# Batch 0's score stacks in the x buffer of batch 1, and two more jobs that score on float32r parts

## The chip, the cores and the metric

The kernel runs on one core of one Trainium2 chip. The metric is the device time of one launch in microseconds, as the median of several runs. Names of engines: PE is TensorE, PEld its weight loads, DVE VectorE, ACT ScalarE, POOL GpSimd, SP SyncE, which issues most DMAs.

## What is computed

Attention with a forget gate over 4 batches, 8 heads, 576 tokens and a head width of 64, then two feed-forward layers over the 2304 tokens, 512 to 2048 to 512 wide. The core of the reference:

```python
scores = (1 / sqrt(64)) * q @ k.T
cum = cumsum(log(clip(f, 1e-4, 1)), axis=-1)
scores = where(causal, -1e9, scores + cum[..., :, None] - cum[..., None, :])
attn = exp(scores - max(scores)); attn = attn / (sum(attn) + 1e-9)
x = (attn @ v).transpose(0, 2, 1, 3).reshape(2304, 512)
h = x @ moe_w_in;  g = h * tanh(softplus(h));  x = g @ moe_w_out
h = x @ moe2_w_in; g = h * cos(h);             out = g @ moe2_w_out
```

Inputs are float32. The kernel keeps their accuracy in matmuls by splitting operands in a high and a low float32r part and summing products of parts.

## The kernel before

**Attention** is cut in jobs of two heads (a head pair). Batch 0 has eight jobs: jobs 0 to 3 are its four head pairs on query blocks 0 and 1 (256 queries, 256 keys), jobs 4 to 7 the same pairs on blocks 2, 3 and 4 (128, 128 and 64 queries, 384, 512 and 576 keys). The text numbers jobs from 0, so the seventh and eighth job are jobs 6 and 7, and job 8 is the first of batch 1. Batches 1 to 3 have four jobs each, with all five blocks. An item is a block of a job. `attention_units` (L365) runs over half items: scores of an item (`scores`, L513) and the weighted sum of an older one (`av`, L622) in the first half, transposes of the item three back (`transposes`, whose copies out of PSUM are L594 on ScalarE and L596 on VectorE) and the normalising (L575 on GpSimd) in the second. Row maxima are taken on VectorE (L558), exponentials on ScalarE (L562).

**Stacks.** A score matmul contracts 128 rows: 64 of q (or k), two rows of the cumulated gate, and constant rows of -1, 0 and 1 that add one and subtract the other. The operands of a job lie in a stack, of which there are two of each kind, used in turn by even and odd jobs. A plain stack is float32: one matmul per head and column range (L521), which runs as two passes. A float32r stack has four parts and takes two float32r matmuls (L527), the second of which adds the products with the low parts. In the kernel before `whole(jb)` says that all jobs of batch 0 are plain. `prep_job` (L430) fills the stack of the next job during the present one: DMAs of the gate rows from `cumd`, transposes by TensorE (L470), and copies out of PSUM. For a plain stack these are ScalarE copies (L494) and one on VectorE (L496). For a float32r stack each run of columns takes, for each head, a ScalarE copy (high part, L501) and a VectorE subtraction (low part, L502), and then a GpSimd copy that duplicates the high part (L507).

**Where the stacks lie.** The plain pair is in a pool of its own. The float32r stack of even jobs (`stkr0`, first used by job 8) lies in the attention pool from the start. The one of odd jobs takes the place of the plain pair: when job 9 is prepared, that pool is closed and the new stack is cleared by `new_stack` (L654) with six GpSimd memsets (L672 to L679), which wait for the last plain scores, those of job 7. In GpSimd's queue five of them stand ahead of the last duplicating copy for job 8.

**Around it.** Matmuls of the first layer's hidden units on finished tokens (`hidden_units`, L164, matmuls L159, copies L184 on ScalarE and L186 on VectorE) fill TensorE between attention's steps; a credit that grows per half item says how many. I call them fills. From the start w_in is converted piece by piece, on VectorE and ScalarE in turn (L127, L129, L135, L139, L141). After attention come the rest of the hidden units, the first layer's output and the second layer, all TensorE work. The order within each engine's queue is not the order of the code alone: the tile framework's list scheduler places each instruction by its own timeline, keeping dependences.

Of the kernel before, what the change touches and what calls it, by code (L numbers as in the profile page):

```python
# [9 lines left out]
F32 = mybir.dt.float32  # L10
# [17 lines left out]
CUT_BATCHES = (0,)  # L28
PAIR_LAG = 3
# [12 lines left out]
def tile_attention_two_ffn(  # L42
# [322 lines left out]
    def attention_units(p, bank):  # L365
# [13 lines left out]

        def span(jb):  # L380
            pi, bl = jobs[jb]
            return divmod(pi, NP) + (QS[bl[0]], QS[bl[-1]] + QR[bl[-1]], bl[-1])

        def load_job(jb):
# [37 lines left out]
        def part(jb, rows, x, j, lo, hi):  # L422
            st, tails = stack(jb)
            if whole(jb) or x % 2:
                return st[x][rows, j, lo:hi]
# [4 lines left out]
        def prep_job(jb):  # L430
# [6 lines left out]
            for row, x in ((96, 0), (64, 1)) if whole(jb) else ((96, 2), (64, 3)):  # L437
# [3 lines left out]
                elif whole(jb):  # L441
# [25 lines left out]
            for g in groups:  # L467
# [6 lines left out]
                for (which, P), run in runs.items():  # L474
# [12 lines left out]
                    if whole(jb):  # L487
# [25 lines left out]
        def scores(jb, i):  # L513
# [5 lines left out]
            def product(o, j, c0, c1):  # L519
                if whole(jb):  # L520
# [12 lines left out]
            if r == 64:  # L533
                heads.append([])
                for c0, c1, mk in ((0, w // 2, maskt[:, 0 : w // 2]), (w // 2, w, mask2[:, 320 - w // 2 : 320])):
                    t = bank()[:, 0 : c1 - c0]
                    for j in (1, 0) if whole(jb) else (0, 1):
                        with ExitStack() as hold:
                            if whole(jb) and j == 0:
                                hold.enter_context(tc.issue_after(marks["score"].ins))  # L540
                            product(t[64 * j : 64 * j + 64] if whole(jb) else t, j, c0, c1)
# [110 lines left out]
        stacks, early = {}, ExitStack()  # L652

        def new_stack(pool, name, dt, en):  # L654
            if dt == F32:
                t = pool.tile([128, 2, 2, S], dt, name=name, bufs=1)
                st, tails = [t[:, 0], t[:, 1]], None
                q, k = st
                nc.gpsimd.memset(q[96:128], 0.0)
                en.memset(q[64:96], -1.0)  # L660
            else:
                t = pool.tile([128, 2 * QW + 4 * S], dt, name=name, bufs=1)
                st, tails = [None] * 4, {}
                for n, x in enumerate((0, 2)):
                    at = n * QW
                    w = QW - TAIL
                    st[x] = t[:, at : at + 2 * w].rearrange("p (j s) -> p j s", j=2)[:, :, 0:TAIL]
                    at += TAIL
                    both = t[:, at : at + 256].rearrange("p (j s) -> p j s", j=2)[:, :, 0:64]
                    tails[x] = (t[:, at : at + 128], t[:, at + 64 : at + 192], both)  # L670
                    if n:
                        en.memset(f(t[64:96, n * QW : n * QW + QW]), -1.0)  # L672
                        nc.gpsimd.memset(f(t[96:128, n * QW : n * QW + QW]), 0.0)
                    nc.gpsimd.memset(f(t[:, at + 64 : at + 128]), 0.0)
                    at = 2 * QW + 2 * S * n
                    st[x + 1] = t[:, at : at + 2 * S].rearrange("p (j s) -> p j s", j=2)
                k = f(st[3])
            nc.gpsimd.memset(k[64:96], 0.0)
            en.memset(k[96:128], 1.0)  # L679
            return st, tails  # L680

        def stack(jb):
            key = (whole(jb), jb % 2)
            if key not in stacks:
                if key == (False, late % 2):
                    early.close()
                    pool = late_sb.enter_context(tc.tile_pool(name="stk", bufs=1))
                else:
                    pool = p
                stacks[key] = new_stack(pool, f"stkr{jb % 2}", F32R, nc.gpsimd)  # L690
# [229 lines left out]
```

## Time and profile before

| | us |
|---|---|
| median of 3 runs | 1022.57 (1022.57 to 1023.02) |
| profiled execution | 1022.4 |
| its span | 1020.6 |
| granted clock of TensorE, mean | 0.998 |
| TensorE busy | 998.3 (98% of the span) |
| VectorE busy | 582.3 |
| ScalarE busy | 539.0 |
| GpSimd busy | 178.6 |

The span is what the trace shows, from the first to the last instruction; the profiled execution has 1.8 us around it. TensorE's share is an average. Attention fills about the first third, and there the engines stand otherwise in each stage; a stage is read by a window of its own.

### The profile page before, as it was taken

To read this page: it belongs to the slowest core of one execution; us is meant where nothing else is said; L and a number is where in the kernel's file an instruction comes from. 1 tells how busy PE (TensorE), PEld (TensorE's weight loads), DVE (VectorE), ACT (ScalarE), POOL (GpSimd) and SP (SyncE) were. 2 spreads that over 40 slices of the span, in tenths; PEclk is the share of its full clock that TensorE was granted. 3 is DMA by queue.
4 is the path that set the end of the run, shared out by engine and by line. 5 is a ranking of instruction groups with operands and counts; after the bars stand their busy time and mean duration, and the time that the engine had idled before them with its cause. 6 is when DMAs were issued, how large, how long until landed. Compare 5 with 4: busy or idle time off the path is not lost.

```text
span 1020.6 us, 16522 instructions
## 1 busy us (share of the span) xinstructions
PE 998.3 (98%) x5852; PEld 855.8 (84%) x5852; DVE 582.3 (57%) x1350; ACT 539.0 (53%) x1158; POOL 178.6 (17%) x255
## 2 busy tenths in 40 slices
PE   5998999999999999999999999999999999999998
PEld 3686899899999999988898888888888888888887
DVE  5867766665555437657662487665544544444454
ACT  5885765665555446557664565544433333333343
POOL 7225432432332200012220031110000000000000
PEclk9999999999999999999999999999999999999999
DMA  5874333233322268848784546102101100100010
GB/s 122 215 205 113 99 88 99 72 95 90 88 71 60 67 224 285 272 139 306 241 293 122 178 147 246 42 1 83 42 1 58 68 1 1 51 32 1 1 42 21
DMA packets 118494, 111.77 MB, mean 110 GB/s; under 512 B 66700, under 2 KB 87180, under 8 KB 118412
## 3 DMA queue, kind: packets, MB, share of 16 engines
q1 hardware_dynamic: 114060, 106.00, 34.0%
q10 hardware_dynamic: 4352, 4.72, 1.4%
q8 instruction: 46, 0.75, 0.3%
q14 instruction: 36, 0.29, 0.1%
HBM read 77.49 MB, written 33.18 MB: 108 GB/s over the span
## 4 chain that ended last, share of the span: by engine, by line
PE 90%; DMA 3%; ACT 3%; POOL 2%; DVE 2%; issue 1%; SPq 0%; POOLq 0%; ACTq 0%; DVEq 0%
PE h L159 24%; PE acc L264 19%; PE hx L159 11%; PE acc L256 11%; PE hx L256 4%; PE h L256 4%; PE s L527 4%; PE s L637 4%; PE s L613 3%; DMA raw<-in_moe_w_in_dram 2%; PE acc L159 2%; PE s L470 2%; ACT s L562 1%; PE s L521 1%; PE s L601 1%
## 5 line engine op out<-in xcount | busy, mean ns | idle before, releaser
L159 PE MATMUL h<-xb,wih 128*128 128x288 f32 (+2 forms) x840 | 180.4, 303 | 2.1 <-DVE hs L186 1.0
L159 PEld LDWEIGHTS h<-xb,wih 128*128 128x128 f32 x840 | 136.2, 188 | 8.7 <-issue 2.1
L159 PE MATMUL h<-xb,wil 128*128 128x288 f32 (+2 forms) x420 | 124.4, 297 | 0.0
L575 POOL TENSOR_SCALAR s<-s,sm 128x128 f32<-128x128 f32 (+4 forms) x144 | 84.3, 598 | 183.0 <-DVE sm L573 121.4
L264 PE MATMUL acc<-woh,gh 128*128 128x512 f32 x288 | 112.9, 392 | 0.0
L264 PE MATMUL acc<-woh,gl 128*128 128x512 f32 x288 | 112.3, 391 | 0.0
L264 PE MATMUL acc<-wol,gh 128*128 128x512 f32 x288 | 112.0, 389 | 0.0
L562 ACT ACTIVATE s<-s,mx 128x128 f32<-128x128 f32 (+4 forms) x144 | 83.6, 581 | 46.4 <-DVE mx L558 45.3
L558 DVE CUSTOM_DVE_ANT_0 s<-s,maskt 128x128 f32<-128x128 f32 (+4 forms) x144 | 67.2, 483 | 55.0 <-PE s L613 24.3
L329 DVE TENSOR_TENSOR gl<-hl,gh 128x512 fp32r<-128x512 f32 x72 | 57.8, 803 | 69.1 <-ACT gh L324 68.8
L315 ACT ACTIVATE n<-n 128x512 f32<-128x512 f32 (+1 forms) x80 | 47.1, 589 | 86.6 <-DVE n L309 86.5
L159 PE MATMUL hx<-x,wih 128*128 128x512 f32 (+1 forms) x320 | 92.7, 369 | 0.0
L159 PE MATMUL h<-x,wih 128*128 128x512 f32 (+1 forms) x320 | 91.0, 369 | 0.0
L329 DVE TENSOR_TENSOR gl<-e,gh 128x512 fp32r<-128x512 f32 (+1 forms) x80 | 53.9, 674 | 51.7 <-ACT gh L324 51.6
L308 DVE TENSOR_SCALAR n<-e 128x512 f32<-128x512 f32 (+1 forms) x80 | 32.7, 408 | 85.3 <-ACT e L301 84.7
L159 PEld LDWEIGHTS h<-xb,wil 128*128 128x128 f32 x420 | 78.8, 188 | 0.8
L324 ACT ACTIVATE gh<-e 128x512 fp32r<-128x512 f32 (+1 forms) x80 | 47.1, 589 | 53.6 <-DVE e L320 50.0
L324 ACT ACTIVATE gh<-hl 128x512 fp32r<-128x512 f32 x72 | 45.1, 627 | 47.5 <-issue 30.2
L256 PE MATMUL acc<-gl,woh 128*128 128x512 f32 (+1 forms) x192 | 67.7, 354 | 0.0
L159 PEld LDWEIGHTS hx<-x,wih 128*128 128x128 f32 x320 | 58.4, 188 | 11.0
L256 PE MATMUL acc<-gh,wol 128*128 128x512 f32 (+1 forms) x192 | 67.6, 354 | 0.0
L159 PEld LDWEIGHTS h<-x,wih 128*128 128x128 f32 x320 | 58.4, 188 | 10.9
(121 smaller groups left out, 2119.7 us busy)
## 6 DMA issues: line engine op xcount, KB each, us to landing
hl<-hd SPq DMA_DIRECT2D x72, 256.0 KB
raw<-in_moe_w_in_dram SPq DMA_DIRECT2D x32, 512.0 KB
raw<-in_moe_w_out_dram SPq DMA_DIRECT2D x32, 512.0 KB
hd<-hs SPq DMA_DIRECT2D x32, 288.0 KB
yd<-stage SPq DMA_DIRECT2D x32, 256.0 KB
x<-yd SPq DMA_DIRECT2D x32, 256.0 KB
natk<-in_k_dram SPq DMA_DIRECT2D x32, 144.0 KB
hd<-hs ACTq DMA_DIRECT2D x16, 288.0 KB
```

The lines of the kernel that those rows point to most:

```text
L159: nc.tensor.matmul(o, lhsT=a[wsl], rhs=b[:, kk, :], start=(kk == 0 and i == 0), stop=(kk == NK - 1 and i == 2),)
L256: nc.tensor.matmul(acc[ti][d][:, 0:T], lhsT=a[dsl], rhs=b[:, gs], start=(start and i == 0), stop=(end and i == 2),)
L264: nc.tensor.matmul(acc[ti][m], lhsT=a[:, ms], rhs=b[:, j % 2, :], start=(start and i == 0), stop=(end and i == 2),)
L308: nc.vector.tensor_scalar(out=t, in0=e, scalar1=ROUND, scalar2=ROUND, op0=ALU.add, op1=ALU.subtract)
L315: nc.scalar.activation(out=t, in_=t, func=AF.Sin, scale=TWO_PI)
L324: gmark[n] = nc.scalar.activation(out=gh, in_=e, func=AF.Copy)
L329: marks["v1"] = nc.vector.tensor_tensor(out=gl, in0=st.pop(n)[0], in1=f(gst[n][0]), op=ALU.subtract)
L527: marks["score"] = nc.tensor.matmul(o, lhsT=tails[x][j] if both else st[x][:, j, QS[i] : w], rhs=st[x + 1][:, j, c0:c1], start=(x == 0 and ...
L558: marks["ttr"] = nc.vector.tensor_tensor_reduce(out=s[:, c0:c1], in0=o, in1=mk, scale=-1.0, scalar=prev, op0=ALU.add, op1=ALU.min, accum_o ...
L562: nc.scalar.activation(out=s[:, 0:w], in_=s[:, 0:w], func=AF.Exp, scale=-1.0, bias=mx, accum_out=sm[:, j : j + 1])
L575: nc.gpsimd.tensor_scalar(out=s[:, 0:w], in0=s[:, 0:w], scalar1=sm[:, j : j + 1], scalar2=1.0, op0=ALU.mult, op1=ALU.mult)
L637: pair = nc.tensor.matmul(t[64 * j : 64 * j + 64, c0:width], lhsT=vt[jb][keys, c, j], rhs=pt[keys, j, c, c0:width], start=(c == 0), stop=( ...
```

## The change

`whole(jb)`, which still says which jobs belong to the cut batch, is joined by `plain(jb)`: true for the first `PLAIN_JOBS = 6` jobs. So jobs 6 and 7 take float32r stacks. The plain pair is laid in the buffer "xb" of batch 1's x, which is first written much later. Both float32r stacks lie in the attention pool from the start. Their clearings, 12 memsets, are collected in a list, and the loop over half items issues one of them per half item from the fifteenth half item on. The preparation of job 6 may start a half item earlier, as its cut form takes more steps.

```diff
 CUT_BATCHES = (0,)
+PLAIN_JOBS = 6
...
+        def plain(jb):
+            return jb < PLAIN_JOBS
...
-                cut = nm == "q" and not whole(jb)
-                P, C = (128, 4) if cut else SPLIT[khi - lo]
+                cut = nm == "q" and not plain(jb)
+                P, C = (128, (TAIL - lo) // 128) if cut else SPLIT[khi - lo]
...
-                if which == 0 and not whole(jb):
-                    cols += [(which, src, 128, 4, c, 128 * c) for c in range(4)] + [(which, src, 64, 1, 4, TAIL)]
+                if which == 0 and not plain(jb):
+                    cols += [(which, src, 128, 4, c, lo + 128 * c) for c in range((TAIL - lo) // 128)]
+                    cols += [(which, src, 64, 1, 4, TAIL)]
                     continue
...
-        stacks, early = 15, ExitStack()
...
+        stacks, clearings = 15, []
+
+        def clear(rows, value):
+            clearings.append((rows, value))
+
+        def small_stack(t, en):
+            q, k = t[:, 0], t[:, 1]
+            nc.gpsimd.memset(q[96:128], 0.0)
+            en.memset(q[64:96], -1.0)
             nc.gpsimd.memset(k[64:96], 0.0)
             en.memset(k[96:128], 1.0)
+            return [q, k], None
+
+        def new_stack(pool, name):
+            t = pool.tile([128, 2 * QW + 4 * S], F32R, name=name, bufs=1)
...
+                if n:
+                    clear(f(t[64:96, n * QW : n * QW + QW]), -1.0)
+                    clear(f(t[96:128, n * QW : n * QW + QW]), 0.0)
+                clear(f(t[:, at + 64 : at + 128]), 0.0)
...
+            clear(k[64:96], 0.0)
+            clear(k[96:128], 1.0)
             return st, tails
 
         def stack(jb):
-            key = (whole(jb), jb % 2)
...
+            return stacks[plain(jb), jb % 2]
+
+        pair = xps[1].tile([128, 2, NK, S], F32, tag="xb", name="stk", bufs=1).rearrange("p a b s -> p (a b s)")
+        pair = pair.rearrange("p (n x j s) -> p n x j s", n=2, x=2, j=2)
         for i in range(2):
-            stacks[True, i] = new_stack(e, f"stk{i}", F32, nc.gpsimd if i else nc.vector)
+            stacks[True, i] = small_stack(pair[:, i], nc.gpsimd if i else nc.vector)
             if i == 0:
                 make_masks()
-        stack(late - 1)
+        for i in range(2):
+            stacks[False, i] = new_stack(p, f"stkr{i}")
+        spread = 2 * NP * len(CUT_BATCHES) - 1
...
-                begin = max(0, 2 * len(bl) - (9 if jb + 1 < len(jobs) and not whole(jb + 1) else 5))
+                begin = max(0, 2 * len(bl) - (9 if jb + 1 < len(jobs) and not plain(jb + 1) else 5))
...
+            if m >= 2 * spread and clearings:
+                rows, value = clearings.pop(0)
+                nc.gpsimd.memset(rows, value)
```

Every other `whole(jb)` inside `load_job`, `part`, `prep_job` and `product` becomes `plain(jb)`; the closing of the removed pools goes as well.

**The order of the queues.** Three places of the queues, as the two programs give them. A row is a line, an operation, its output and inputs, and partitions by elements. Numbers behind a name tell buffers apart: s_... are PSUM banks, stk the plain stacks (stk_126 the second of them before), stkr_131 and stkr_1315 the float32r stacks of even and odd jobs before, and stkr_127 and stkr_128 those of even and odd jobs after. Lines after the change are 5 to 6 higher, and those of `hidden_units` one.

GpSimd at the start, between the plain stacks' clearings and the first normalise, before:

```order
L679 MEMSET stk_126 32x1152
L674 MEMSET stkr_131 128x64
L672 MEMSET stkr_131 32x1216
L673 MEMSET stkr_131 32x1216
L678 MEMSET stkr_131 32x1152
L679 MEMSET stkr_131 32x1152
L750 AFFINE_SELECT maskt<-maskt 128x128
L756 AFFINE_SELECT mask_85<-mask_85 64x64 x2
L674 MEMSET stkr_131 128x64
L575 TENSOR_SCALAR s<-s,sm 128x128 x2
```

And with the change:

```order
L746 MEMSET stkr_127 128x64
L746 MEMSET stkr_127 32x1216 x2
L746 MEMSET stkr_127 32x1152 x2
L746 MEMSET stkr_128 128x64
L746 MEMSET stkr_128 32x1216 x2
L756 AFFINE_SELECT maskt<-maskt 128x128
L762 AFFINE_SELECT mask_85<-mask_85 64x64 x2
L746 MEMSET stkr_128 32x1152 x2
L746 MEMSET stkr_127 128x64
L746 MEMSET stkr_128 128x64
L580 TENSOR_SCALAR s<-s,sm 128x128 x2
L580 TENSOR_SCALAR s<-s,sm 128x256 x2
```

All 12 clearings of the float32r stacks stand at the start of GpSimd's queue, eight of them ahead of the mask; before there were five ahead and one behind.

ScalarE around the exponential of job 7's last item (128x576), while job 8's stack is filled, before:

```order
L501 ACTIVATE stkr_131<-s_1179 64x192
L501 ACTIVATE stkr_131<-s_1131 64x64
L501 ACTIVATE stkr_131<-s_1179 64x192
L184 ACTIVATE hs<-h 128x256
L501 ACTIVATE stkr_131<-s_1131 64x384 x2
L594 ACTIVATE p<-s_1235 128x4x2x64
L594 ACTIVATE p<-s_1241 64x2x64
L562 ACTIVATE s,sm<-s,mx 128x576
```

And with the change:

```order
L506 ACTIVATE stkr_127<-s_1224 64x192
L506 ACTIVATE stkr_127<-s_1176 64x64
L599 ACTIVATE p<-s_1284 128x4x2x64
L567 ACTIVATE s,sm<-s,mx 128x576
L506 ACTIVATE stkr_127<-s_1224 64x192
L506 ACTIVATE stkr_127<-s_1176 64x384
L599 ACTIVATE p<-s_1290 64x2x64
L506 ACTIVATE stkr_127<-s_1176 64x384
```

The exponential stood behind all stack copies of job 8; now it and a transpose's copy (p) stand ahead of the last four, with the 384-column copies of both heads at the end.

TensorE from job 7's last scores to job 8's first, with the change:

```order
L532 MATMUL s_1242<-stkr_128 128x288 x4
L532 MATMUL s_1247<-stkr_128 128x288 x4
L160 MATMUL h<-xb,wih_1234 128x256 x4
L606 MATMUL s_1284<-ident,s 128x128 x4
L160 MATMUL h<-xb,wil_1235 128x256
L160 MATMUL h<-xb,wih_1234 128x256 x2
L160 MATMUL h<-xb,wil_1235 128x256 x2
L160 MATMUL h<-xb,wih_1234 128x256 x2
L160 MATMUL h<-xb,wil_1235 128x256
L609 MATMUL s_1290<-ident,s 64x128
L532 MATMUL s_1312<-stkr_127 128x128 x4
```

Before, 15 fills stood between the same transposes (then L601 and L604) and job 8's first scores; now the eight after L606 do, four more having moved ahead of it. On GpSimd the five memsets ahead of job 8's last duplicating copy are gone from this place, and one normalise (128x576) stands there.

## Rows read from the trace of the kernel before

**Rows 1.** The page: busy times, and the chain that ended last, by engine.
```profile
PE 998.3 (98%) x5852; PEld 855.8 (84%) x5852; DVE 582.3 (57%) x1350; ACT 539.0 (53%) x1158; POOL 178.6 (17%) x255
...
PE 90%; DMA 3%; ACT 3%; POOL 2%; DVE 2%; issue 1%; SPq 0%; POOLq 0%; ACTq 0%; DVEq 0%
```

**Rows 2.** Windows: length, busy PE, PEld, DVE, ACT, POOL (x count), PEclk, DMA share, GB/s.
```profile
20.00:30.00 10.00, 8.66 (x37) 6.02 (x37) 6.90 (x24) 8.02 (x22) 4.23 (x8) 1.00 0.75 178
...
40.00:50.00 10.00, 9.36 (x62) 5.77 (x58) 8.64 (x30) 9.29 (x24) 4.52 (x7) 1.00 0.87 227
...
50.00:89.20 39.20, 39.20 (x316) 31.05 (x315) 30.20 (x88) 29.74 (x74) 12.36 (x18) 1.00 0.65 176
...
90.00:100.00 10.00, 6.64 (x46) 5.03 (x46) 4.90 (x18) 4.54 (x12) 7.15 (x9) 0.83 0.31 88
...
96.00:97.00 1.00, 1.00 (x8) 0.72 (x9) 0.62 (x5) 0.29 (x1) 0.23 (x2) 0.50 0.00 0
```

**Rows 3.** Timeline before job 8's first scores: start, us, engine, line [idle before <- releaser].
```profile
89.94 1.11 POOL L672 MEMSET stkr<- 32x1216 f32 x1
...
92.02 0.50 PE L159 MATMUL h<-xb,wih 128*128 128x256 f32 x2 [1.00 <-DVE hs L186]
...
94.47 0.82 POOL L507 CAST stkr<-stkr 64x768 fp32r<-64x768 f32 x1
...
95.34 0.89 PE L527 MATMUL s<-stkr 128*128 128x128 f32 x4 [2.35 <-POOL stkr L507]
```

**Rows 4.** Timeline: loads at plain scores of 512 columns, float32r scores, and fills.
```profile
63.51 0.19 PEld L521 LDWEIGHTS s<-stk 128*128 128x128 f32 x1 [0.24 <-issue]
...
64.37 0.19 PEld L159 LDWEIGHTS h<-xb,wih 128*128 128x128 f32 x1 [0.24 <-issue]
...
86.73 0.40 PE L159 MATMUL h<-xb,wih 128*128 128x256 f32 x2
...
87.08 0.40 PE L159 MATMUL h<-xb,wih 128*128 128x256 f32 x2
...
128.11 0.63 PE L527 MATMUL s<-stkr 128*128 128x512 f32 x2
...
128.57 0.45 PE L159 MATMUL h<-xb,wih 128*128 128x320 f32 x2
```

**Rows 5.** Timeline before and after job 7's last scores: stack copies, transposed weights, exponential, casts.
```profile
88.71 0.33 ACT L501 ACTIVATE stkr<-s 64x192 fp32r<-64x192 f32 x1 [0.53 <-DVE stkr L502]
...
89.16 0.50 POOL L507 CAST stkr<-stkr 64x384 fp32r<-64x384 f32 x1 [0.64 <-ACT stkr L501]
...
90.43 0.49 ACT L501 ACTIVATE stkr<-s 64x384 fp32r<-64x384 f32 x1 [0.62 <-DVE stkr L502]
...
90.94 0.75 ACT L594 ACTIVATE p<-s 128x512 f32<-128x512 f32 x2
90.95 0.56 DVE L502 SCALAR_TENSOR_TENSOR stkr<-s,stkr 64x384 fp32r<-64x384 f32 x1
...
91.59 0.77 ACT L562 ACTIVATE s<-s,mx 128x576 f32<-128x576 f32 x1
```

**Rows 6.** VectorE by line and form, 50 to 89.2 us: us busy, mean ns.
```profile
L496 DVE TENSOR_SCALAR stk<-s 64x320 f32<-64x320 f32 x2 | 0.9, 469 | 0.0
...
L502 DVE SCALAR_TENSOR_TENSOR stkr<-s,stkr 64x192 fp32r<-64x192 f32 x2 | 0.7, 352 | 0.1
...
L502 DVE SCALAR_TENSOR_TENSOR stkr<-s,stkr 64x64 fp32r<-64x64 f32 x2 | 0.4, 223 | 0.1
```

**Rows 7.** Timeline of the start: GpSimd's clearings, mask and normalise; four plain passes, twice.
```profile
9.82 1.10 POOL L672 MEMSET stkr<- 32x1216 f32 x1
...
13.74 2.07 PE L521 MATMUL s<-stk 128*128 128x256 f32 x4
...
14.35 0.29 POOL L750 TENSOR_SCALAR_AFFINE_SELECT maskt<-maskt 128x128 f32<-128x128 f32 x1
...
17.09 0.73 POOL L575 TENSOR_SCALAR s<-s,sm 128x128 f32<-128x128 f32 x2 [1.74 <-ACT s L562]
...
31.73 1.03 PE L521 MATMUL s<-stk 128*128 128x256 f32 x4
```

More of the change, by code (lines that the diff above doesn't have):

```diff
@@ L423, in part @@
             st, tails = stack(jb)
-            if whole(jb) or x % 2:
+            if plain(jb) or x % 2:
                 return st[x][rows, j, lo:hi]
@@ L436, in prep_job @@
             h0 = b * H + 2 * hp
-            for row, x in ((96, 0), (64, 1)) if whole(jb) else ((96, 2), (64, 3)):
+            for row, x in ((96, 0), (64, 1)) if plain(jb) else ((96, 2), (64, 3)):
                 if jb == 0:
@@ L440, in prep_job @@
                         nc.sync.dma_start(out=st[x][row + y : row + y + 1], in_=cums[y][h0 : h0 + 2])
-                elif whole(jb):
+                elif plain(jb):
                     nc.sync.dma_start(out=st[x][row : row + 2], in_=cumd[h0 : h0 + 2].rearrange("h y s -> y h s"))
@@ L486, in prep_job @@
                     sc = 0.125 if which == 0 else 1.0
-                    if whole(jb):
+                    if plain(jb):
                         for j in range(2):
@@ L519, in product @@
             def product(o, j, c0, c1):
-                if whole(jb):
+                if plain(jb):
                     marks["score"] = nc.tensor.matmul(
@@ L536, in scores @@
                     t = bank()[:, 0 : c1 - c0]
-                    for j in (1, 0) if whole(jb) else (0, 1):
+                    for j in (1, 0) if plain(jb) else (0, 1):
                         with ExitStack() as hold:
-                            if whole(jb) and j == 0:
+                            if plain(jb) and j == 0:
                                 hold.enter_context(tc.issue_after(marks["score"].ins))
-                            product(t[64 * j : 64 * j + 64] if whole(jb) else t, j, c0, c1)
+                            product(t[64 * j : 64 * j + 64] if plain(jb) else t, j, c0, c1)
                     heads[0].append((t, c0, c1, mk))
@@ L650, in av @@
             nc.vector.tensor_tensor(out=xl, in0=t[:, 0:width], in1=f(xh), op=ALU.subtract)
[L652 to L677, printed above, removed]
@@ L678, in new_stack @@
+        stacks, clearings = {}, []
+        def clear(rows, value):
[4 more added lines that the diff above has]
+            en.memset(q[64:96], -1.0)
             nc.gpsimd.memset(k[64:96], 0.0)
             en.memset(k[96:128], 1.0)
+            return [q, k], None
+        def new_stack(pool, name):
+            t = pool.tile([128, 2 * QW + 4 * S], F32R, name=name, bufs=1)
+            st, tails = [None] * 4, {}
+            for n, x in enumerate((0, 2)):
+                at = n * QW
+                w = QW - TAIL
+                st[x] = t[:, at : at + 2 * w].rearrange("p (j s) -> p j s", j=2)[:, :, 0:TAIL]
+                at += TAIL
+                both = t[:, at : at + 256].rearrange("p (j s) -> p j s", j=2)[:, :, 0:64]
+                tails[x] = (t[:, at : at + 128], t[:, at + 64 : at + 192], both)
+                if n:
+                    clear(f(t[64:96, n * QW : n * QW + QW]), -1.0)
+                    clear(f(t[96:128, n * QW : n * QW + QW]), 0.0)
+                clear(f(t[:, at + 64 : at + 128]), 0.0)
+                at = 2 * QW + 2 * S * n
+                st[x + 1] = t[:, at : at + 2 * S].rearrange("p (j s) -> p j s", j=2)
+            k = f(st[3])
+            clear(k[64:96], 0.0)
+            clear(k[96:128], 1.0)
@@ L680, in new_stack @@
             return st, tails
         def stack(jb):
-            key = (whole(jb), jb % 2)
[L684 to L690, printed above, removed]
-            return stacks[key]
-        late = 1 + max(jb for jb in range(len(jobs)) if whole(jb)) + 1
@@ L796, in tile_attention_two_ffn @@
         xps[i] = xsb[i].enter_context(tc.tile_pool(name=f"x{i}", bufs=1, side="right"))
-    att_sb, att_ps, late_sb = ExitStack(), ExitStack(), ExitStack()
+    att_sb, att_ps = ExitStack(), ExitStack()
     ap = att_sb.enter_context(tc.tile_pool(name="att", bufs=2, side="right"))
@@ L840, in tile_attention_two_ffn @@
     att_ps.close()
-    late_sb.close()
     att_sb.close()
```

1 line of the change is left out of this document (removed).

## The prediction

> **What bounds the kernel now.** The page comes first: TensorE is busy 98% of the span, and 90% of the chain that ended last is its own work [rows 1]. So an edit counts by the TensorE work that it takes away and by the holes that it opens or closes in TensorE's queue; work of other engines counts where TensorE ends up waiting for it. The windows then show where that share is not 98% [rows 2]. From 50 to 89.2 us TensorE has no gap (39.20 of 39.20) and is the bound. In 20 to 30 it is busy 8.66 of 10 and in 40 to 50 9.36, with ScalarE at 9.29 and VectorE at 8.64: there a mixture bounds. In 90 to 100 it is busy only 6.64, and the granted clock is 0.83, in 96 to 97 0.50.
>
> The timeline names that hole [rows 3]. TensorE idles 1.00 us for VectorE's copy of a hidden unit (the fill at 92.02), then 2.35 us for GpSimd's duplicating copy, ahead of job 8's first scores at 95.34. That copy starts at 94.47, behind memsets that clear the next stack, job 9's, from 89.94 on. The clock at 0.83 over ten us costs another 10 x 0.17 = 1.7.
>
> **Scores of jobs 6 and 7.** Removed are plain scores. One 512-column block takes four passes for two heads. Weight loads follow TensorE's pace, and two passes lie between 63.51 and 64.37, so four take 1.72 [rows 4]. A float32r block of 512 columns takes 128.57 - 128.11 = 0.46 for a head, 0.92 for two. The block gains 0.80; one of 384 columns three quarters of that, 0.60. The last block (64 queries) runs eight passes either way and I count it zero, as I do the transposes of q (three for four). For each job 1.4, for two **-2.8**, on TensorE's path, which has no gap there.
>
> **Filling their stacks.** For each job VectorE does, for two heads, subtractions of 64, 192, 256 and 384 columns, and drops a copy of 320. By 0.22, 0.35 and 0.47 [rows 6] and 0.56 [rows 5], with 0.42 for the 256 columns as an estimate between 0.35 and 0.56, that is 2 x (0.22 + 0.35 + 0.42 + 0.56) - 0.47 = 2.6, 5.3 for both jobs. VectorE is busy 30.20 of 39.20 us there [rows 2]; it would be 35.5 of 36.4, which just fits. ScalarE gains three copies a job, 2 x 0.2 + 2 x 0.4 less one of 0.4, 0.8: 29.74 becomes 31.3. GpSimd gains four duplicating copies a job at 0.3 to 0.8 (0.50 and 0.82 are shown [rows 3, 5]), some 4.4, on 12.36. SP issues two more DMAs a job; they are asked for at the previous job's start, so that job covers them, and without that cover scores would wait for the gate rows. I count all of this at nothing on the path, except the copies that end last:
>
> **The hole at job 8 closes.** The five memsets ahead of the copy go. I count the two waits, **-3.35**, and keep the clock's 1.7 as it is, since new waits stand nearby.
>
> **New waits.** The order of ScalarE shows the exponential of the last item ahead of job 8's last stack copies. Behind TensorE's transposes L606 this chain runs: transposed weights 0.49 (the larger share of 0.75 for two copies, the other 0.26), exponential 0.77, a copy of 192 columns 0.33, one of 384 0.49, VectorE's subtraction 0.56, which the second head's copy waits for, that copy 0.49, GpSimd's duplicate 0.82 [rows 3, 5]. Sum 3.95. TensorE has eight fills and a transpose to run meanwhile: three fills take 0.35 (86.73 to 87.08 [rows 4]), so 0.95, and the transpose about 0.15, an estimate from a fill's 0.12. The wait is 3.95 - 1.1 = 2.85; 2.2 if half of the VectorE step and a copy overlap otherwise, 3.6 if each step adds 0.1 of signalling. At job 7 the same runs with 192 columns last: 0.49 + 0.26 + 0.77 + 0.33 + 0.35 + 0.33 + 0.50 = 3.03 against twelve fills and the transpose, 1.55: 1.5, with 0.8 to 2 as bounds. Together **+4.4**. Queued behind these scores on TensorE stand the next sums of weights and values and more fills; VectorE's maxima and ScalarE's exponentials of jobs 7 and 8 start as much later.
>
> **The start.** The clearings are not spread: GpSimd's order has all 12 at the program's start. A 64-column one and two of 1216 more stand ahead of the mask, 0.2 + 2 x 1.1 = 2.4 by the row at 9.82 [rows 7], so the mask comes at 16.8 for 14.35. Behind the mask stand two of 1152 columns and one of 64 more, at 1.1 each and 0.2; the first normalise, at 17.09 before, cannot start before 20.3, **3.2 later**. What of it reaches the end? None, if the work that waits anyway (conversions on ScalarE and VectorE, transfers) is done in the gap, or all 3.2, as transposes wait for that normalise. I take 0.8, nearer to none: TensorE is idle 1.34 of ten us in 20 to 30 and 0.64 in 40 to 50 [rows 2], waits into which a shifted chain can sink.
>
> The clock at the start: the granted clock reads 1.00 in 20 to 30 [rows 2], but the same four passes take 2.07 at 13.74 and 1.03 at 31.73 [rows 7], a ratio of two, as between 1.2 and 2.4 GHz. The sum has no term for a longer slow start, the third rival has. The Trainium skill (TensorE: Matmul & The Clock Gate, Part 1) says that the throttled clock is the default and that activity releases it, which speaks against a change that thins out TensorE's start. By that rule the trace's durations agree, its clock column doesn't.
>
> **Sum.** -2.8 - 3.35 + 4.4 + 0.8 = **-0.95**. The profiled execution took 1022.4 (span 1020.6 and 1.8 around it), so 1021.45; the median of the runs, 1022.57, is 0.17 above it: **1021.6 us**. About 0.2%, 2.05 us, is what a measurement can tell from no change, and this lies within it.
>
> **Rivals.**
> - *The new waits are half and the clock stays up* (faster). The scheduler orders by its own times; if ScalarE is earlier on the chip than in its plan, half of 4.4 falls away, and with no hole of 3.35 the clock doesn't fall to 0.50, 1.7 more. -0.95 - 2.2 - 1.7 = -4.85: 1017.7. For it: GpSimd's 4.4 us of clearing in the middle are certainly gone. Against it: the order is fixed in the queues, and the exponential does stand ahead.
> - *VectorE becomes the bound of jobs 6 and 7* (slower). At 35.5 of 36.4 us any subtraction that waits for its ScalarE copy delays what stands behind it, among it the copies of hidden units that free the fills' banks. Place: 70 to 95 us. Price: the 2.8 of the scores is lost and the wait of 1.00 for such a copy, counted as gone, stays: -0.95 + 2.8 + 1.0 = +2.85, 1025.4. It decides once VectorE costs TensorE more than 0.95 + 2.05 = 3.0. For it: 97%. Against it: in 50 to 89.2 VectorE already stood at 77% without one gap on TensorE.
> - *The clearings' delay passes in full* (slower). 3.2 in place of 0.8 gives +1.45, 1024.0, still within 0.2%. If TensorE also stays that much longer at the level of the 2.07 us [rows 7], half of 3.2 more is lost: +3.05, 1025.6. Against it: the idle of 20 to 50 us, into which it can sink.
> - *The change does not do what it says.* For the spreading this is so by the order, and it is in the sum.
>
> **How the numbers follow.** The forecast and its near variants, the delay in full among them: 0.44; the first rival and cases on its side: 0.34; the VectorE rival 0.13, the start with the slow clock 0.05, mixtures of the two 0.04. So faster by over 0.2% 0.34, within 0.2% 0.44, slower 0.22. The range takes in the rivals: 1017.5 to 1025.6. Below it lies the case that the new waits hardly arise (-0.95 - 4.4 - 1.7 = -7.05, 1015.5), above it VectorE's loss and the full start together; I give these two in ten. The forecast's own range is 1020.5 to 1024.
>
> **What would show it.** Right: in 90 to 100 no memset on GpSimd, and TensorE's hole moved to a wait of some 3 us for the duplicating copy ahead of job 8's scores, with one of 1.5 at job 7; four passes of jobs 6 and 7 in 0.92; the mask 2.4 us later and the first normalise at about 20.3; job 4's scores about 1 us later than before. Wrong: no wait ahead of job 8's scores, a clock of 1.00 through 90 to 100, VectorE without a gap from 70 on, or TensorE's start shifted by the whole 3.2.

## The result, and the profile after

The change makes the kernel slower: 1028.61 us, median of 6 runs (1027.47 to 1029.43), against 1022.57 of 6 runs before, a ratio of 1.0051 (95% interval 1.0040 to 1.0061). That is +6.0 us where the forecast was -0.95, and above the range.

The profiled execution, the slowest of the six, took 1029.43 us with a span of 1027.7, 7.1 more than before. The page, beside [rows 1]:

```profile
PE 999.5 (97%) x5850; PEld 859.4 (84%) x5850; DVE 588.3 (57%) x1364; ACT 540.0 (53%) x1164; POOL 181.5 (18%) x263
...
PE 88%; DMA 3%; ACT 3%; DVE 3%; POOL 2%; issue 1%; ACTq 0%; POOLq 0%; SPq 0%; DVEq 0%
```

TensorE is busy no shorter (999.5 us for 998.3) although the scores of jobs 6 and 7 take shorter passes, and its share of the chain fell. The windows after, same columns as [rows 2]:

```profile
20.00:30.00 10.00, 8.05 (x34) 5.32 (x33) 6.10 (x26) 8.00 (x24) 4.33 (x10) 1.00 0.60 131
40.00:50.00 10.00, 9.13 (x66) 5.89 (x65) 8.85 (x28) 9.37 (x24) 2.60 (x4) 1.00 0.79 212
50.00:89.20 39.20, 34.80 (x260) 28.24 (x260) 30.31 (x86) 26.50 (x68) 15.10 (x22) 0.92 0.60 162
80.00:90.00 10.00, 7.15 (x40) 5.36 (x41) 5.72 (x18) 5.54 (x15) 3.92 (x6) 0.66 0.26 76
90.00:100.00 10.00, 8.72 (x73) 7.67 (x70) 8.67 (x26) 8.15 (x21) 3.27 (x5) 1.00 0.74 191
100.00:110.00 10.00, 7.87 (x62) 6.54 (x63) 7.12 (x21) 4.00 (x13) 2.90 (x5) 0.83 0.37 110
...
84.00:85.00 1.00, 1.00 (x3) 1.00 (x4) 0.00 (x0) 0.53 (x1) 0.00 (x0) 0.50 0.00 0
```

The stretch from 50 to 89.2 us, which had no gap, now has 4.4 us of them. The clock is lowered twice, at half in the middle of each stretch (0.50 in 84 to 85 and in 104 to 105): by the windows that takes 10 x 0.34 = 3.4 us in 80 to 90 and 10 x 0.17 = 1.7 in 100 to 110, where before there was one such stretch of 1.7. Both go with waits. From the list of TensorE's waits, by line and releaser (total us, times, longest):

```profile
PE s L532 <- POOL stkr L512: 6.1, 2, 3.3
```

Where the time went is seen best from when each job's first scores start, in us, from TensorE's timeline. The numbered experiments are below; row 11 is the change once more, and the last column is the span.

| | job 4 | job 5 | job 6 | job 7 | job 8 | span |
|---|---|---|---|---|---|---|
| before | 35.67 | 44.44 | 57.74 | 73.80 | 95.34 | 1020.6 |
| the change | 36.65 | 45.93 | 67.07 | 83.95 | 102.13 | 1027.7 |
| 1, all eight plain | 36.38 | 45.71 | 58.93 | 76.80 | 95.88 | 1021.9 |
| 2, clearings held | 35.44 | 44.60 | 66.56 | 81.58 | 100.08 | 1025.7 |
| 3, exponential late | 36.09 | 45.50 | 66.48 | 82.32 | 99.11 | 1023.2 |
| 4, matmuls in the waits | 37.00 | 46.34 | 67.34 | 84.28 | 103.85 | 1026.0 |
| 5, copies of a bank first | 36.13 | 45.74 | 61.63 | 76.00 | 94.28 | 1017.9 |
| 6, the same in the kernel before | 35.66 | 45.28 | 58.57 | 74.63 | 94.47 | 1018.3 |
| 7, the same for jobs 6, 7 | 36.60 | 45.69 | 61.50 | 77.64 | 97.24 | 1022.5 |
| 8, the same, all eight plain | 36.16 | 45.83 | 59.07 | 76.27 | 95.84 | 1018.6 |
| 9, 5 and early clearings | 36.23 | 45.02 | 60.89 | 75.23 | 91.81 | 1016.0 |
| 11, the change again | 36.14 | 45.43 | 66.29 | 82.31 | 100.52 | 1025.6 |
| 12, 9 with all eight plain | 36.48 | 44.75 | 58.05 | 74.30 | 93.66 | 1016.8 |

The two traces of the change differ by 0.5 us at job 4, 0.8 at job 6 and 1.6 at job 8, so smaller differences between two rows say little. At job 8 the change is 6.8 us behind (5.2 in row 11), with the same 156 fills done: nearly the whole loss is there. The largest step in the table is at job 6, 9.3 us later, but 55 more fills run ahead of it (102 for 47 in the order). At 0.117 us each, an estimate from [rows 4], these are 6.4 us of work that is only done earlier. What is lost shows in TensorE's idle time, by windows from job to job: up to job 4, on to job 6, to job 7 and to job 8 it is 13.5, 1.5, 3.8 and 3.4 us, for 12.9, 0.6, 0.0 and 3.4 before. That is 5.4 of the 6.8 us, most of it between jobs 6 and 7.

Ahead of job 6 TensorE does not wait for the stack: the last subtraction for it ends at 65.09, and fills run until 67.07. But the fill of this float32r stack has become long. In the timeline of the change between 50 and 68 us, ScalarE's copies and VectorE's subtractions for it, start and length first:

```profile
50.44 0.36 ACT L506 ACTIVATE stkr<-s 64x256 fp32r<-64x256 f32 x1
...
52.80 0.42 DVE L507 SCALAR_TENSOR_TENSOR stkr<-s,stkr 64x256 fp32r<-64x256 f32 x1
...
53.64 0.38 ACT L506 ACTIVATE stkr<-s 64x256 fp32r<-64x256 f32 x1
...
54.64 0.43 DVE L507 SCALAR_TENSOR_TENSOR stkr<-s,stkr 64x256 fp32r<-64x256 f32 x1
...
57.18 0.21 ACT L506 ACTIVATE stkr<-s 64x64 fp32r<-64x64 f32 x1
...
59.09 0.22 DVE L507 SCALAR_TENSOR_TENSOR stkr<-s,stkr 64x64 fp32r<-64x64 f32 x1
...
60.61 0.22 ACT L506 ACTIVATE stkr<-s 64x64 fp32r<-64x64 f32 x1
...
62.24 0.23 DVE L507 SCALAR_TENSOR_TENSOR stkr<-s,stkr 64x64 fp32r<-64x64 f32 x1
62.50 0.33 ACT L506 ACTIVATE stkr<-s 64x192 fp32r<-64x192 f32 x1
...
63.29 0.35 DVE L507 SCALAR_TENSOR_TENSOR stkr<-s,stkr 64x192 fp32r<-64x192 f32 x1
...
64.00 0.33 ACT L506 ACTIVATE stkr<-s 64x192 fp32r<-64x192 f32 x1
64.46 0.60 POOL L512 CAST stkr<-stkr 64x384 fp32r<-64x384 f32 x1 [0.59 <-ACT stkr L506]
64.73 0.36 DVE L507 SCALAR_TENSOR_TENSOR stkr<-s,stkr 64x192 fp32r<-64x192 f32 x1
```

All these copies and subtractions read one PSUM bank. The code writes, head by head, a copy and then a subtraction, and the second head's copy waits for the first head's subtraction, although both only read the bank. In the rows no such copy starts before the subtraction ahead of it has ended (53.64 behind 53.22, 60.61 behind 59.31, 64.00 behind 63.64). Where it cost ScalarE idle time it stands in the list of the change's ScalarE waits:

```profile
ACT stkr L506 <- DVE stkr L507: 4.7, 9, 1.7
```

Each instruction takes 0.2 to 0.4 us, but between two of them each engine does what else stands in its queue, so the six pairs run from 50.44 to 65.1. The plain fill of the same stack before had no such chain: five ScalarE copies ran in one block of 2.14 us from 54.38 on.

The waits for the duplicating copy come where the prediction put them. The change's timeline ahead of job 7's first scores:

```profile
81.16 0.77 ACT L567 ACTIVATE s<-s,mx 128x576 f32<-128x576 f32 x1
...
81.92 0.31 ACT L506 ACTIVATE stkr<-s 64x192 fp32r<-64x192 f32 x1
...
82.43 0.35 DVE L507 SCALAR_TENSOR_TENSOR stkr<-s,stkr 64x192 fp32r<-64x192 f32 x1
...
82.81 0.33 ACT L506 ACTIVATE stkr<-s 64x192 fp32r<-64x192 f32 x1 [0.58 <-DVE stkr L507]
...
83.40 0.50 POOL L512 CAST stkr<-stkr 64x384 fp32r<-64x384 f32 x1
...
83.95 1.65 PE L532 MATMUL s<-stkr 128*128 128x384 f32 x4 [2.85 <-POOL stkr L512]
```

The exponential, then the two copies with VectorE between them, then GpSimd: 2.85 us of idle TensorE. Ahead of job 8 it is 3.30.

### The profile page after: what moved, and what is told of

It is laid out like the page before. It is cut to its first block, busy times and chain, and to the rows that moved or that the text cites. A ratio compares the mean times of both kernels' runs of the same rounds, so it can differ in the third digit from the quotient of the medians.

```text
span 1027.7 us, 16539 instructions
## 1 busy us (share of the span) xinstructions
PE 999.5 (97%) x5850; PEld 859.4 (84%) x5850; DVE 588.3 (57%) x1364; ACT 540.0 (53%) x1164; POOL 181.5 (18%) x263
## 4 chain that ended last, share of the span: by engine, by line
PE 88%; DMA 3%; ACT 3%; DVE 3%; POOL 2%; issue 1%; ACTq 0%; POOLq 0%; SPq 0%; DVEq 0%
PE h L160 24%; PE acc L265 19%; PE hx L160 11%; PE acc L257 10%; PE s L532 4%; PE h L257 4%; PE hx L257 4%; PE s L642 4%; PE s L618 3%; DMA raw<-in_moe_w_in_dram 2%; PE acc L160 2%; PE s L475 2%; ACT s L567 1%; DMA yd<-stage 1%; PE s L526 1%
## 5 line engine op out<-in xcount | busy, mean ns | idle before, releaser
L532 PE MATMUL s<-stkr 128*128 128x288 f32 (+3 forms) x320 | 67.2, 327 | 7.5 <-POOL stkr L512 6.1
```

The source lines that it names most:

```text
L532: marks["score"] = nc.tensor.matmul(o, lhsT=tails[x][j] if both else st[x][:, j, QS[i] : w], rhs=st[x + 1][:, j, c0:c1], start=(x == 0 and ...
```

## The experiments

Three theories were set against each other. **A**: the late place of the last exponential and the clock that falls behind each wait make the loss. **B**: the clearings at the program's start make it. **C**: the filling of the float32r stacks, with its hand-overs between ScalarE and VectorE, sets the pace of jobs 6 to 8, and idle TensorE and half clock follow from it. The kernel before was run again beside each set of experiments, and its median differed (1022.6 to 1023.8), so ratios to it are what is compared. The change has 1.0051. Each edit also lets the scheduler place everything else anew, so two versions differ in more than the edited lines.

**1. All eight jobs plain, the rest of the change kept.**

```diff
-PLAIN_JOBS = 6
+PLAIN_JOBS = 8
```

> All eight jobs of batch 0 plain again (PLAIN_JOBS = 8), the rest of the change kept: stacks in batch 1's buffer, both float32r stacks from the start, 12 clearings at the program's start. Theory A (the waits for the last stack copies of jobs 7 and 8 and the half clock after each make the loss): no wait at job 7, and at job 8 neither the memsets of before nor the late copies; about 1019 us, the start's loss of 1.6 kept. Rival B (the clearings at the start make the loss): 1027 or more, as with the change. Rival C (VectorE is the bound while jobs 6 and 7 are filled): 1019 to 1021, as A; the fourth kernel tells A from C.

(The fourth kernel named there is experiment 3.) Measured: 1024.01 us, ratio 1.0003 (0.9993 to 1.0012), no difference from before. So the loss comes with the float32r scores of jobs 6 and 7, which speaks against B. But A's 1019 and C's 1019 to 1021 were missed too: the wait at job 8 is gone and nothing is won. TensorE's idle time up to job 8 is 16.8 us, as before (16.9), for it now has other gaps, one of them

```profile
76.80 1.56 PE L526 MATMUL s<-stk 128*128 128x384 f32 x4 [1.34 <-ACT stk L499]
```

so attention's own chain can hold TensorE up with plain jobs as well.

**2. Each clearing queued behind a normalise, so that they are spread.**

```diff
-                nc.gpsimd.memset(rows, value)
+                with tc.issue_after(marks["norm"].ins):
+                    nc.gpsimd.memset(rows, value)
```

> The change, with each clearing queued behind the last normalise traced before it, so that GpSimd's queue really spreads them (after job 3's items). Theory A: the start's 1.6 us come back, and the waits at jobs 7 and 8 stay, 1025.5 to 1027 us. Rival B: nearly the whole loss comes back, 1022.5 us or less. Rival C: 1027, as A. The first normalise is at about 17 us again, the mask at 14.4.

Measured: 1029.23, ratio 1.0061 (1.0044 to 1.0078), above what any of the three theories said. The mask comes at 9.60 and the first normalise at 14.73, earlier than expected, and job 4 starts 0.7 to 1.2 us earlier than in the two traces of the change. But in GpSimd's timeline of this kernel the spread clearings now stand between job 6's duplicating copies:

```profile
54.32 1.06 POOL L747 MEMSET stkr<- 32x1152 f32 x1
55.44 0.61 POOL L512 CAST stkr<-stkr 64x512 fp32r<-64x512 f32 x1
...
59.48 1.06 POOL L747 MEMSET stkr<- 32x1152 f32 x1
60.59 0.28 POOL L512 CAST stkr<-stkr 64x128 fp32r<-64x128 f32 x1
```

At job 6 nothing is left of it (66.56, for 67.07 and 66.29), and the runs show no gain at the end. With experiment 1, in which the clearings stand at the start and nothing is lost, B falls as the main cause.

**3. The last exponential of jobs 6 and 7 behind the next job's stack copies** (the exponential is issued after the preparation is drained, behind its copies on ScalarE).

```diff
...
+                if m2 < M and late_exp:
+                    for _ in prep:
+                        pass
+                    with ExitStack() as hold:
+                        for c in copies[-8:]:
+                            hold.enter_context(tc.issue_after(c.ins))
+                        late_exp.pop()()
```

> The change, with the exponential of the last item of jobs 6 and 7 queued behind the next job's stack copies on ScalarE; nothing else moves on ScalarE or TensorE. Theory A: each of the waits for the duplicating copy loses the exponential's 0.9 us, to 1.9 and 2.4, so 1.8 less, about 1026.8 us, and more, down to 1023, if the clock then stays up behind one of them. Rivals B and C: no change, 1028.6.

Measured: 1025.33, ratio 1.0019 (1.0008 to 1.0029): 3.2 thousandths, 3.3 us, less than the change. The waits are 1.78 and 2.49 us, near what A said, and the clock still falls, to 0.83 in 80 to 90 and in 100 to 110:

```profile
82.32 0.97 PE L533 MATMUL s<-stkr 128*128 128x384 f32 x4 [1.78 <-POOL stkr L513]
...
99.11 0.66 PE L533 MATMUL s<-stkr 128*128 128x128 f32 x4 [2.49 <-POOL stkr L513]
```

A is a part of the cause: what stands in the chain that ends with the duplicate counts. It is not all of it, and job 6 still starts at 66.48.

**4. Matmuls on ready data in the waits.**

```diff
+                            with tc.issue_after(marks["tail"].ins):
+                                for _ in range(WARM[jb]):
+                                    nc.tensor.matmul(
+                                        t[:, 0:256], lhsT=W[1, 0, "i"][0][:, 0, 0:128], rhs=xb[0][:, 0, 0, 0:256],
+                                        start=True, stop=True,
+                                    )
```

> The change, with matmuls on data that lies ready (20 ahead of job 7's first scores, 24 ahead of job 8's, 256 columns each, 0.117 us apiece) between the last transpose and the scores that wait; their sums go to the scores' own bank and are overwritten. The waits stay, but TensorE is busy in them. Theory A with the clock as its larger part: the windows from 80 to 90 and 100 to 110 us show a clock of 1.00, and 3.4 + 1.7 us come back: 1023.5 us. If the clock is not part of it (A without the clock, B, C): 1028.6 or a little more.

Measured: 1027.90, ratio 1.0045 (1.0030 to 1.0060). The clock is 1.00 throughout, and yet of 5.1 us at most some 0.6 came back, which the intervals (1.0045 here, 1.0051 for the change) do not tell from nothing. The windows of this kernel:

```profile
80.00:90.00 10.00, 9.03 (x77) 7.94 (x76) 6.86 (x22) 6.38 (x17) 3.94 (x6) 1.00 0.31 84
90.00:100.00 10.00, 7.66 (x70) 7.04 (x68) 7.63 (x24) 7.61 (x20) 3.35 (x5) 1.00 0.84 215
100.00:110.00 10.00, 9.87 (x91) 8.41 (x90) 7.22 (x26) 6.16 (x19) 2.36 (x5) 1.00 0.25 59
```

In job 7 TensorE at full clock is done sooner and then waits, by the timeline, for a VectorE subtraction of the next stack:

```profile
95.37 1.42 PE L533 MATMUL s<-stkr 128*128 128x288 f32 x8 [2.34 <-DVE stkr L508]
```

In the change the same scores start at 95.44. From job 7's first scores to these it is 11.09 us here and 11.49 and 11.51 in the two traces of the change. So of the 3.4 us that the clock takes in job 7 some 0.4 were on the path: A's second half falls there, and C stands. Ahead of job 8 the added matmuls outlast the wait (its scores start at 103.85, for 102.13 and 100.52). From there to the end this trace takes 922.2 us and those of the change 925.5 and 925.1, as if the clock did cost from job 8 on; but other kernels, in which it does not fall there, lie between 922.8 and 926.0, so this is not shown.

**5. The change, with all ScalarE copies out of a bank first, then all VectorE subtractions.**

```diff
                         nc.scalar.activation(out=hi, in_=i_, func=AF.Copy, scale=sc)
-                        nc.vector.scalar_tensor_tensor(
-                            out=dest(lo_r, lo_x, j), in0=i_, scalar=sc, in1=f(hi), op0=ALU.mult, op1=ALU.subtract
-                        )
+                        later.append((dest(lo_r, lo_x, j), i_, sc, hi))
...
+                for o, i_, sc, hi in later:
+                    nc.vector.scalar_tensor_tensor(
+                        out=o, in0=i_, scalar=sc, in1=f(hi), op0=ALU.mult, op1=ALU.subtract
+                    )
```

> The change, with prep_job's cut path written in another order, for all jobs that take it: first all ScalarE copies out of a PSUM bank, then all VectorE subtractions from it, so that a bank goes once from ScalarE to VectorE and not after each head. The work is the same. Theory C (the filling of the float32r stacks, a chain of hand-overs between ScalarE and VectorE with other work of both queued between them, sets the pace of jobs 6 to 8; idle TensorE and its half clock follow from it): job 6's first scores start at about 60 us for 67, no wait above 1 us for a duplicating copy, the clock stays at 1.00, 1020 to 1022 us. Theory A (the place of the exponential, and the clock): the exponential also stands behind the copies here, so 1025 us as with the fourth kernel. Theory B (the start): 1028.6.

(The fourth kernel named there is experiment 3.) Measured: 1019.80, ratio 0.9970 (0.9960 to 0.9980): 8 thousandths below the change, with the same instructions. In its timeline the fill of job 6's stack runs in blocks:

```profile
50.08 0.38 ACT L506 ACTIVATE stkr<-s 64x256 fp32r<-64x256 f32 x1
...
51.50 1.54 ACT L506 ACTIVATE stkr<-s 64x256 fp32r<-64x256 f32 x5
51.95 1.87 POOL L510 CAST stkr<-stkr 64x512 fp32r<-64x512 f32 x3 [0.82 <-ACT stkr L506]
...
53.80 2.07 DVE L512 SCALAR_TENSOR_TENSOR stkr<-s,stkr 64x256 fp32r<-64x256 f32 x6
...
57.58 1.13 DVE L512 SCALAR_TENSOR_TENSOR stkr<-s,stkr 64x384 fp32r<-64x384 f32 x2
...
61.63 0.69 PE L534 MATMUL s<-stkr 128*128 128x384 f32 x3
...
72.00 0.97 ACT L506 ACTIVATE stkr<-s 64x384 fp32r<-64x384 f32 x2
...
77.95 0.77 ACT L569 ACTIVATE s<-s,mx 128x576 f32<-128x576 f32 x1
```

The bank whose copies and subtractions took from 50.44 to 65.1 is done at 55.9; the two subtractions at 57.58 are of the other bank. Job 6 starts at 61.63, no wait for a duplicating copy is left in the list of waits, and the clock is 1.00 in the ten-us windows up to 120 us. This is C's forecast, with a time just below its 1020 to 1022. The last two rows show that the exponential (77.95) stands behind the next stack's copies here too, so A's part is in the gain. Experiment 3, where it also stands there and copies and subtractions still alternate, has 1.0019. Against that the order of the copies gives 4.9 thousandths, which A does not explain.

**6. The kernel before, with the same order of copies.**

> The kernel before, with the same order of copies and subtractions. There the jobs with float32r stacks are jobs 8 to 19, which have five blocks and more TensorE work to hide a fill. Theory C: little to gain, 1021 to 1023 us; so what the order of copies gives the change is the cost of filling stacks in the short jobs. If the kernel before gains as much as the change (5 us or more), the hand-overs cost everywhere, and C for jobs 6 to 8 falls.

Measured: 1019.92, ratio 0.9970 (0.9957 to 0.9983). It gains 3 thousandths, more than the 1021 to 1023 us that C gave it, less than the 5 us that would have felled it. The hand-overs cost before too; in its trace the hole ahead of job 8 [rows 3] has no wait for the duplicating copy any more. The new order gives the change 8 thousandths, so 5 more, which is the whole of its loss.

**7. That order for the stacks of jobs 6 and 7 alone.**

```diff
+                        later.append((dest(lo_r, lo_x, j), i_, sc, hi))
+                        if jb not in (6, 7):
+                            low(*later.pop())
...
+                for x in later:
+                    low(*x)
```

> The change, with that order for the stacks of jobs 6 and 7 alone; from job 8 on copies and subtractions alternate as before. Theory C: most of the gain of the first kernel of this set, 1021 to 1024 us; job 6's first scores at about 60 us, the wait at job 7 gone, some wait at job 8 left. Theory A: the exponential again stands ahead of job 8's last copy, so that wait stays, 1026 us.

Measured: 1024.31, ratio 1.0007 (0.9997 to 1.0016). This is just above C's 1021 to 1024 and below A's 1026. Of the 8 thousandths 4.4 lie in the stacks of jobs 6 and 7. The rest lies from job 8 on, whose stack is still filled head by head, with the exponential ahead of its last copy. This kernel's timeline has there

```profile
97.24 1.12 PE L540 MATMUL s<-stkr 128*128 128x128 f32 x4 [3.96 <-POOL stkr L518]
```

**8. All eight jobs plain, with that order.**

> The change with all eight jobs plain (PLAIN_JOBS = 8) and that order for jobs 8 to 19. Against the first kernel of this set it says what float32r scores in jobs 6 and 7 are worth when their stacks are filled without the hand-overs: by the prediction's 2.8 us of passes it should be 1 to 3 us slower than that kernel. If it is faster, the float32r scores of jobs 6 and 7 cost more than they give in any order of the copies. Theory C says 1022 to 1024 us.

Measured: 1020.59, ratio 0.9972 (0.9961 to 0.9983), not to be told from experiment 5; the 1 to 3 us expected between the two are not there, nor C's 1022 to 1024. TensorE's busy time is 996.5 us here and 994.2 there: 2.3 us of passes are saved. But between 50 and 100 us it is idle 2.4 us here and 3.6 there. The window of this kernel:

```profile
50.00:100.00 50.00, 47.64 (x377) 37.16 (x375) 36.02 (x109) 36.39 (x91) 17.32 (x23) 1.00 0.64 172
```

And that of experiment 5:

```profile
50.00:100.00 50.00, 46.44 (x383) 38.75 (x381) 43.36 (x129) 37.85 (x98) 20.39 (x31) 1.00 0.65 176
```

VectorE does 7.3 us more there (43.36 for 36.02). That this is the price is argued, not shown; it fits experiment 5's list of waits, in which fills stand for converted weights that ScalarE and VectorE deliver later:

```profile
PE h L160 <- ACT wih L140: 1.0, 2, 0.8
...
PE h L160 <- DVE wil L142: 0.7, 2, 0.4
```

In the list of the all-plain kernel the first has 0.2 us and the second is missing. The change itself has this window, with less of VectorE's time in it than experiment 5:

```profile
50.00:100.00 50.00, 44.32 (x335) 36.70 (x334) 39.34 (x112) 34.65 (x89) 18.60 (x27) 0.93 0.62 165
```

**9. Experiment 5, and the clearings behind the normalises of the first items,** from the first half item on, so that they are done before job 6's stack is filled.

```diff
-            if m >= 2 * spread and clearings:
+            if clearings and "norm" in marks:
                 rows, value = clearings.pop(0)
-                nc.gpsimd.memset(rows, value)
+                with tc.issue_after(marks["norm"].ins):
+                    nc.gpsimd.memset(rows, value)
```

> The order of copies and subtractions of the first kernel of the last set (ScalarE's copies of a bank first), and the 12 clearings queued one by one behind the normalises of the first items, done before job 6's stack is filled. Theory B in its small form (the clearings' delay at the start passes to the end in part): job 4's first scores at 35.5 us for 36.1, and 0.5 to 1.5 us less than that kernel, 1018.5 to 1019.5 us. If the delay sinks into other waits: no change, 1019.8 us.

Measured: 1018.75, ratio 0.9952 (0.9937 to 0.9966), the fastest version that computes the whole reference: some 5 us under the kernel before. It lies 1.05 us under experiment 5 by medians and 1.8 by ratios, and the two intervals overlap; with all jobs plain the same step, from experiment 8 to 12, gives 1.3 thousandths. The first normalise starts at 14.74, but the expected 35.5 for job 4 did not come: its scores start at 36.23, for 36.13 in experiment 5. The trace is ahead only later (0.7 us at job 6, 2.5 at job 8), so a gain of about 1 us is likely, and the way it takes is open. In the change the first normalise starts at 21.30, behind the mask and the last clearings, by GpSimd's timeline of the change:

```profile
16.85 0.29 POOL L756 TENSOR_SCALAR_AFFINE_SELECT maskt<-maskt 128x128 f32<-128x128 f32 x1
...
17.57 2.60 POOL L746 MEMSET stkr<- 32x1152 f32 x4
21.30 2.42 POOL L580 TENSOR_SCALAR s<-s,sm 128x128 f32<-128x128 f32 x4 [1.13 <-DVE sm L577]
```

**10. Experiment 5, with one float32r matmul for two in jobs 6 and 7.** The second matmul, which is left out there, carries the products with k's low part and the rows of the gate; those with q's low part are in the first.

```diff
-                for x in (0, 2):
+                xs = (0,) if whole(jb) else (0, 2)
+                for x in xs:
...
-                        start=(x == 0 and not (both and j)), stop=(x == 2 and not (both and not j)),
+                        start=(x == 0 and not (both and j)), stop=(x == xs[-1] and not (both and not j)),
```

> The order of copies and subtractions of that kernel, and jobs 6 and 7 score with one float32r matmul for two: the products with the low parts are left out there, so those scores are less exact. It takes some 2.6 us more of passes off TensorE (0.46 for each 512 columns of a head, three quarters of that for 384, about 0.5 for the last block, by job). If TensorE is the bound of jobs 6 and 7 once the hand-overs are gone: 1017.2 us. Theory C (a chain on other engines sets the pace there, so saved passes come back as idle time): 1019 to 1020 us, with 2 us more of idle TensorE between 50 and 100 us.

Measured: 1017.20, ratio 0.9932 (0.9917 to 0.9946): by medians 2.6 us under experiment 5, by ratios 3.9, no less than the 2.6 of passes. The window has no more idle time than experiment 5's (3.44 us for 3.56):

```profile
50.00:100.00 50.00, 46.56 (x394) 39.20 (x393) 45.72 (x135) 40.34 (x104) 21.94 (x34) 1.00 0.70 187
```

With the hand-overs gone TensorE bounds these jobs after all, and C's last clause, that saved passes come back as idle time, was wrong there. What float32r scores save in passes (experiment 8) is then lost on the side of filling the stacks; that is an inference from these two.

**11. The change again, beside 9 and 10.**

> The change itself, beside these kernels on one chip: 1.005 of the kernel before by every theory; with its job 6 at 67 us, waits of some 3 us for the duplicating copy at jobs 7 and 8 and two stretches at half clock.

Measured: 1028.80, ratio 1.0047 (1.0031 to 1.0063), as before.

**12. Experiment 9 with all eight jobs plain.**

> The first kernel of the last set (copies of a bank first, clearings behind the first items' normalises), with all eight jobs of batch 0 plain. Against it this is what float32r scores in jobs 6 and 7 are worth where the hand-overs and the start are out of the way: by the passes alone 2.8 us, so 1021.5 us here; if the stacks' filling still takes part of it, 1019.5 to 1021; if it takes all, 1018.8.

(The first kernel named there is experiment 9.) Measured: 1018.78, ratio 0.9959 (0.9945 to 0.9972), as experiment 9, and the last of the three cases. Float32r scores in jobs 6 and 7 are worth nothing that these runs can tell, in either order of the clearings. Job 7 starts at 74.30 without a wait; the wait of 1.34 us ahead of it in experiment 1, and one of 1.05 in experiment 8, stand only in the two plain kernels with the clearings at the start.

## Why the prediction was wrong

- **The step that failed is "Filling their stacks".** It summed each engine's added work, found that it "just fits" and counted "all of this at nothing on the path, except the copies that end last". The work was sized well (VectorE's busy time rose by 6.0 us in all, 5.3 were forecast for the two jobs). What was missed is that the copies and subtractions alternate, so that the whole fill is a chain, and not only its end, where "New waits" did count a subtraction that a copy waits for. Job 6's fill ran for 15 us, and its scores came 9 later, behind 55 more fills; between jobs 6 and 7 TensorE then idled 3.8 us for none before. Busy shares can't show this; the wait was visible in [rows 5], as ScalarE's 0.53 and 0.62 us for VectorE's subtraction. Experiments 5 and 6 show it: without the alternation change and kernel before are equal (0.9970 both). The exponential's place moves along in experiment 5; alone it gives 3.2 of the 8.1 thousandths (experiment 3).
- **The new waits** were rightly placed, and 6.15 us (2.85 and 3.30) against 4.4. The cover, sized by the fills in the order, held at job 8 (1.0 us for 1.1) and was longer at job 7 (2.1 for 1.55). The chain took longer at both: from the end of the four transposes to the end of the duplicate 4.3 us for 3.95 at job 8, and 5.0 for 3.03 at job 7, where ScalarE came to the transposed weights only at 80.51, 1.6 us behind these transposes. That the exponential stands in it was right (experiment 3).
- **The clock** was left at 1.7, "since new waits stand nearby"; it fell twice, 5.1 us by the windows. Of the 3.4 in job 7 some 0.4 were a loss (experiment 4); the 1.7 behind job 8's wait are as much as before.
- **The scores** save 2.3 us of busy time for a forecast of 2.8. In the change this was lost in waits. Without the hand-overs it is 0 to 0.8 us by the medians of experiments 5, 8, 9 and 12, not to be told from nothing; fills wait for weights instead.
- **The hole at job 8** did close, but -3.35 was not got: experiment 1 has no such wait, plain jobs and the time of before. Its TensorE idles as long up to job 8, in other places: 1.34 us ahead of job 7 for a copy of a plain stack, a wait that is gone with other clearings (experiment 12). What else takes the hole's place is open.
- **The start** was 0.8 of 3.2. The mask came at 16.85 (16.8 forecast), the first normalise at 21.30 (20.3), job 4 0.5 to 1.0 us late. Experiment 9 gets 1 to 1.8 us back, near the edge of the noise and not by an earlier job 4, so the size fits and the path is not shown.
- **The rivals.** The one in which VectorE becomes the bound, +2.85, had the right place and was too small, with the wrong reason: from 50 to 100 us VectorE is busy 39.3 us in the change and 43.4 in experiment 5, which is faster by 8 thousandths. Its order was the cost, not its load. The start with the slow clock, +3.05, was as near in size and is not what happened: experiment 1 has the same start and no loss.

## What to carry to other kernels

When a step hands a buffer back and forth between two engines, count the hand-overs, and price each with what else stands in both queues, not with the instructions' own lengths: here six pairs of 0.2 to 0.4 us took 15 us. Write such a step with all of one engine's work on a buffer first. A wait that the profile names may stand in front of another chain of nearly the same length, so price its removal with what is late next; and where work is moved to another unit, test the plain form beside it once the order is mended: here the new order was worth 3 thousandths without the change, and the float32r scores added nothing to it.

## What was not expected of the hardware

The clock fell at waits in which TensorE did nothing (2.85 and 3.30 us in the change), to a mean of 0.66 and 0.83 in ten us, and stayed at 1.00 where the same waits held matmuls (experiment 4). The length of a wait alone does not tell: the 2.34 us in experiment 4 left it at 1.00, and in experiment 3 it read 0.83 in the ten us with the wait of 1.78. At job 7 it had fallen to 0.50 in 83 to 84, before the wait was over; at job 8 TensorE had worked again for about a us (1.00 in 102 to 103, 0.66 in 103 to 104). The Trainium skill (TensorE: Matmul & The Clock Gate, Part 1) has the throttled clock as what TensorE returns to without activity; the traces agree, with 0.50 in 83 to 84 behind two us without work. What was not expected is how little this may cost: of the 3.4 us that the lowered clock takes in job 7 by the window, matmuls in the wait brought back some 0.4 at its last scores, since another chain was later.
